# Scan and routing operands in a PSUM bank, one pair of score banks, the third state sum behind qq, and half the zero products

## The chip, the cores and the metric

The program runs on one core of one Trainium2 chip. The metric is the device time of one execution in microseconds (us), 836.23 in the median of three runs (836.04 to 836.23). The clock is that of the whole program: a linear attention, a layer of eight experts behind a router, and a dense feed-forward layer, one after the other.

## The reference

Inputs are q, k, v and alpha of shape (4, 8, 768, 48) and the weights of both layers, all float32.

```python
def _attn_ref(q, k, v, alpha):
    for t in range(S):                       # S = 768 steps, one 48 x 48 state per batch and head
        state = alpha[:, :, t, :, None] * state + einsum('bhd,bhe->bhde', k[:, :, t], v[:, :, t])
        y[:, :, t] = einsum('bhd,bhde->bhe', q[:, :, t], state)

def _moe_ref(x, w_gate, w1, w2):             # x is y as 3072 tokens of 384
    expert_idx = np.argmax(x @ w_gate, axis=1)
    ...                                      # gate_w: softmax probability of the chosen expert
    out[mask] = gate_w[mask, None] * (np.maximum(xe @ w1[e], 0.0) @ w2[e])   # for each of 8 experts

def _moe2_ref(x, w_in, w_out):
    h = np.maximum(x @ w_in, 0.0)
    return h * h @ w_out
```

## The kernel before

**Tiling.** The 32 pairs (batch, head) times two are 16 pairs of heads, and the 768 steps are two halves of three chunks of 128 steps. That makes NU = 32 units; units 0 to 15 are the first halves, units 16 to 31 the second. A tile of one unit is 112 rows (48 of one head at row 0, 48 of the other at row 64) by 3 x 128 steps. The state between chunks is carried by matrices of 112 x 48.

**One unit's work.** `scan` (line 181, VectorE) makes the running products of alpha within each chunk, A; it reads the loaded tile `qka` and `rst`, a tile of 112 x 387 that restarts the product at each chunk and bounds it from below. `prep_a` (188 to 190, ScalarE) makes 1/A as exp(-ln A). `prep_p` (199 and 200, GpSimd from unit 2 on) makes M = k/A and the product R = A/A, from which `prep_k` (205, VectorE) makes the corrected key kk; `prep_q` (210, VectorE) makes qq = q times A. `scores` (225, TensorE) multiplies kk and qq chunk by chunk, `masked` (232, VectorE) applies the causal mask to the product and writes pt. `ktr` transposes kk (241, TensorE; ScalarE copies it to kn, 242). `state_pe` (252, TensorE) makes kn times v per chunk, and `state_0` to `state_4` carry the state through the chunks: `add` (261, VectorE) writes T = product + state, `decay` (257, ScalarE) scales T. The first halves make three sums (called below the first, second and third state sum; a first half's first one needs no addition, so its additions are those of `state_1` and `state_3`), the second halves two. `yout` (289 and 293, TensorE; copy to yt on ScalarE, 295) makes the output, `xout` (312, TensorE) turns it to token rows and adds the router's logits: ScalarE copies the rows (314), VectorE adds the logits (321, 323).

**Zero products.** `fill` issues FILL matmuls of a tile of zeros, 384 columns each, into the score tile ahead of the scores, and into py ahead of `yout`. The real products overwrite them.

**Order.** All engines run the order in which the code is written. In pass u of the loop over units, in the order of the code: kk and qq of unit u+2, scores and transposes of unit u+1, `xout` of unit u-1, mask of u+1, preparation of u+4, `yout` of u, state of u+1, scan of u+5. Every fourth pass from u = 5 on has `route_a` (347 to 359), seven small VectorE instructions that turn logits of four units into one-hot rows and running counts, behind the scan; two passes later `route_b` (368, 369) makes two ranking matmuls and `route_s` the slots to which GpSimd scatters the rows (384). In passes 28 to 30 the first weights of the experts are split into two parts, ScalarE (125) and VectorE (126), at the end of the pass.

**PSUM.** It has eight banks of 512 float32 per row here. The pool `ps_s` has two slots of two banks, tag `sc`, which the score tile takes in turn; the pool `ps_1` has one bank each for `pk`, `st`, `py` and `px`. The router's matmuls share `px`.

Behind the loop the experts and the dense layer run as one dense sequence of matmuls on TensorE (lines 453, 483, 791).

Of the kernel before, what the change touches and what calls it, by code (L numbers as in the profile page):

```python
# [8 lines left out]
F32 = mybir.dt.float32  # L9
# [4 lines left out]
ALU = mybir.AluOpType  # L14
# [6 lines left out]
CH = 128  # L21
# [9 lines left out]
NE = 8  # L31
# [11 lines left out]
CVW = 256  # L43
TINY = 2.0 ** -50
KC = 3
FILL = 2
BLK = 512
PRE = (28, 28, 28, 29, 29, 29, 30, 30)
NBLK = TOK // BLK
# [22 lines left out]
def main_path(tc, qka, v, vt, wg, wts, wf64, cst, out):  # L72
# [24 lines left out]

    def warm(n, pool, tag, x):

        pw = pool.tile([128, 2, 512] if tag == "sc" else [128, 512], F32, tag=tag, name="pw")  # L100
        pw = (pw[:, 0, :] if tag == "sc" else pw)[:, 0:384]
        for _ in range(n):
            nc.tensor.matmul(pw, x[:, 0:128], x[:, 0:384], start=True, stop=True)

# [38 lines left out]

    wi = one.tile([112, NP, 104], F32, name="wi")
    smid = one.tile([112, NPAIR, 48], F32, name="smid")
    rst = one.tile([112, HC, CH + 1], F32, name="rst")
    neg = one.tile([112, 1], F32, name="neg")
    junk = one.tile([112, HC, CH], F32, name="junk")
    zr = one.tile([128, HS], F32R, name="zr")
# [1 line left out]
    tri = one.tile([128, 128], F32R, name="tri")  # L151
    onr = one.tile([128, 128], F32R, name="onr")
    ohx = [one.tile([128, NE, HC + 1], F32R, name=f"ohx{i}") for i in range(2)]
    rone = one.tile([128, NE * (HC + 1)], F32, name="rone")

    st = {}
    SP = ((0, 64), (64, 112))

# [58 lines left out]

    def scores(u):
        kk, qq = st[u, "k"], st[u, "q"]
        sc = ps_s.tile([128, 2, 512], F32, tag="sc", name="sc")  # L220
        fill(sc[:, 0, 0:HS], FILL)
        for j in range(HC):
            cs = slice(j * CH, (j + 1) * CH)
            for x in range(2):
                nc.tensor.matmul(sc[:, x, cs], kk[64 * x:64 * x + 48, cs], qq[64 * x:64 * x + 48, cs], start=True, stop=True, skip_group_check=True)  # L225
        st[u, "sc"] = sc
# [103 lines left out]
    def cv(o):  # L330
        return ct[:, o:o + HC * NE].rearrange("p (i e) -> p i e", e=NE)
# [4 lines left out]
    def col(n):  # L336
        return sm.tile([128, HC, 1], F32, tag=n, name=n)
# [4 lines left out]

    def route_a(g):
        lg = st[g, "lg"]
        mx, wm = col("mx"), col("wm")
        eq, w = t3("eq"), t3("w")
        nc.vector.tensor_reduce(mx, lg, axis=AX.X, op=ALU.max)
        nc.vector.tensor_tensor(eq, lg, bc(mx), op=ALU.is_equal)
        nc.vector.tensor_tensor(w, eq, cv(C_WROW), op=ALU.mult)
        nc.vector.tensor_reduce(wm, w, axis=AX.X, op=ALU.max)  # L350
        oh, ohn = ohx[g % 2], ohx[(g + 1) % 2]
        ohv = oh[:, :, 1:].rearrange("p e i -> p i e")
        nc.vector.tensor_tensor(ohv, w, bc(wm), op=ALU.is_equal)
        cum = sm.tile([128, NE, HC + 1], F32R, tag="cum", name="cum")
        nc.vector.tensor_tensor_scan(cum.rearrange("p e i -> p (e i)"), rone, oh.bitcast(F32).rearrange("p e i -> p (e i)"), 0.0, op0=ALU.mult, op1=ALU.add)
        if g < 2 * B - 1:
            nc.vector.tensor_copy(ohn[:, :, 0:1], cum.bitcast(F32)[:, :, HC:HC + 1])
        else:
            nc.vector.tensor_copy(cnt[:, 0:NE], cum.bitcast(F32)[:, :, HC])
        if g == GA - 1:  # L360
            nc.vector.tensor_copy(cnt[:, NE:NE + 1], cum.bitcast(F32)[:, 0, HC:HC + 1])
        st[g, "rt"] = ohv, cum, mx
# [139 lines left out]
    with tc.manual_schedule():  # L502
        load(0)
        load(1)
        nc.scalar.preload_act_table_set("natural_log_exp_and_others")
        nc.vector.memset(rst, 2.0 ** -60)
        nc.vector.memset(rst[:, :, 0:1], 1.0)
        nc.gpsimd.memset(zt, 0.0)
        nc.gpsimd.memset(zr.bitcast(F32), 0.0)
        nc.gpsimd.memset(neg, -1.0)  # L510
        nc.gpsimd.memset(chk, 0.0)
        nc.gpsimd.memset(wi, 0.0)
        nc.gpsimd.memset(ones, 1.0)
        for u in range(2, 6):
            load(u)
            if u == 2:
                for x in range(2):
                    nc.sync.dma_start(wi[64 * x:64 * x + 48, :, 96:104], wg.rearrange("(p x e) g -> x e p g", p=NP, x=2)[x])
        warm(8, ps_s, "sc", zt)
        scan(0)  # L520
        prep_a(0)
        prep_p(0)
        prep_k(0)
        prep_q(0)
        scan(1)
        prep_a(1)
        scan(2)
        prep_p(1)
        prep_a(2)
        prep_p(2)  # L530
        scores(0)
        ktr(0)
        warm(7, ps_1, "py", zt)
        masked(0)
        prep_k(1)
        prep_q(1)
        scan(3)
        prep_a(3)
        prep_p(3)
        state_pe(0)  # L540
        state_0(0)
        for x, r in enumerate((0, 64)):
            nc.vector.tensor_copy(wi[r:r + 48, :, x * 48:x * 48 + 48], ct[r:r + 48, r:r + 48].rearrange("p (a c) -> p a c", a=1).to_broadcast([48, NP, 48]))
        nc.vector.tensor_copy(tri, ct[:, C_TRI:C_TRI + 128])
        nc.vector.tensor_copy(onr, ones)
        nc.vector.memset(rone, 1.0)
        nc.vector.memset(rone.rearrange("p (e i) -> p e i", e=NE)[:, :, 0:1], 0.0)
        nc.vector.tensor_copy(ohx[0][:, :, 0], ct[:, C_EC:C_EC + 8])
        scan(4)
        xsv = xs.rearrange("(e r) d -> e r d", e=NE)[:, 0:C].rearrange("e (p j) d -> e p j d", p=ZP)  # L550
        nz, ns, ready = 0, 0, 0
        for u in range(NU):
            if u + 6 < NU:
                load(u + 6)
            if u >= 2 and nz < 2 * NE:
                for _ in range(2):
                    nc.sync.dma_start(xsv[nz // 2, :, nz % 2 * 2:nz % 2 * 2 + 2], zt[0:ZP].rearrange("p (j d) -> p j d", j=1).to_broadcast([ZP, 2, XW]))
                    nz += 1
            if u + 2 < NU:
                prep_k(u + 2)  # L560
                state_1(u)
                prep_q(u + 2)
            else:
                state_1(u)
            if u + 1 < NU:
                scores(u + 1)
                ktr(u + 1)
            state_2(u)
            g, gs = divmod(u - NP - 1, NP)
            if u > 0:  # L570
                xout(u - 1)
            if u + 1 < NU:
                masked(u + 1)
            state_3(u)
            if u + 4 < NU:
                prep_a(u + 4)
            state_4(u)
            if u + 4 < NU:
                prep_p(u + 4)
            yout(u)  # L580
            if 14 <= u < 22:
                wload(0, (u - 14) // 4, nc.scalar, (u - 14) % 4)
            rs = gs + (g == 2 * B - 2)
            if g >= 0 and rs == 2:
                route_b(g)
            if u + 1 < NU:
                state_pe(u + 1)
            if u + 5 < NU:
                scan(u + 5)
            if u + 1 < NU:  # L590
                state_0(u + 1)
            if g >= 0 and rs == 2:
                route_s(g)
                ready = g + 1
            if g >= 0:
                if gs == 0:
                    route_a(g)
            for k, x in enumerate(PRE):
                if u == x:
                    split_step(0, k, 8)  # L600
            for _ in range(2 if u >= 28 else 1):
                if u >= 9 and ns < min(ready, GA if u <= 28 else 2 * B) * HC:
                    scatter(ns)
                    ns += 1
            if u == 28:
                assert ns == GA * HC
                xload(0)
                wload(1, 0)
        while ns < ready * HC:
            scatter(ns)  # L610
            ns += 1

        pts = [ps_s.tile([128, 2, 512], F32, tag="sc", name="xt0")[:, 0, :], ps_1.tile([128, 512], F32, tag="st", name="xt1"), ps_1.tile([128, 512], F32, tag="pk", name="xt2")]
        pts = xtr_pe(0, pts)
        fill(banks(0)[0][:, 0:HS], 2)
        xout_a(NU - 1)
        xsp(0, 0, pts[0])
        xsp(0, 1, pts[1])
        xsp(0, 2, pts[2])
        xout_b(NU - 1)  # L620
        st["xl"] = e0p.tile([PARTS[0][3], PARTS[0][2] // PARTS[0][3], NE + 1], F32, name="xl", bufs=1)
        nc.vector.tensor_copy(st["xl"], st["xr", 0][:, :, DM:XW])
        g = 2 * B - 1
        route_a(g)
        g1a(0, 0)
        g1a_pe(0, 1)
        route_b(g)
        route_s(g)
        while ns < 2 * B * HC:
            scatter(ns)  # L630
            ns += 1
        g1a_act(0, 1)
        for npre in range(len(PRE), 10):
            split_step(0, npre, 8)
        npre = max(10, len(PRE))
# [503 lines left out]
```

## Time and profile before

| what | us |
|---|---|
| median of three runs | 836.23 |
| the profiled execution | 836.37 |
| its span from first to last instruction | 834.4 |
| TensorE busy | 819.3 |
| VectorE busy | 570.8 |
| ScalarE busy | 394.5 |
| GpSimd busy | 291.4 |
| units 3 to 30, from the fill of unit 3's scores to that of unit 31's | 30.40 to 168.00 |

The profile has a page of totals and a trace that can be asked for stretches. A row of the time line names the start and the length in us, the engine, the line, the operation, what it writes and reads, and how many such instructions it holds; a bracket gives the idle time of the engine ahead of it and what ended that. Rows of TensorE with several matmuls are pipelined: the start of the next row tells when the engine took up the next work, better than the length does. PE is TensorE, DVE VectorE, ACT ScalarE, POOL GpSimd.

### The profile page before, as it was taken

The numbers are of one execution on the slowest core, as the hardware profiler recorded it, in microseconds if no ns is written. First come the engines' busy times: TensorE is split into PE (matmuls) and PEld (weight loads), VectorE is DVE, ScalarE is ACT, GpSimd is POOL, SyncE is SP. The second block draws the span as 40 slices with busy tenths as digits, with TensorE's granted clock in tenths as the row PEclk, the third lists the DMA queues.
The fourth block names the chain that finished last, engine by engine and source line by source line (L and its number), as shares of the span: only waits on it lengthen the run. The fifth ranks groups of instructions, "written<-read, shape, count | busy, mean of one in ns | idle before, by whom it ended". The sixth has DMA issues, their size and how long they took to land.

```text
span 834.4 us, 14539 instructions
## 1 busy us (share of the span) xinstructions
PE 819.3 (98%) x5412; PEld 731.9 (88%) x5412; DVE 570.8 (68%) x1085; ACT 394.5 (47%) x885; POOL 291.4 (35%) x310
## 2 busy tenths in 40 slices
PE   8999999999999999999999999999999999999996
PEld 5777777789999999999989999999998999999996
DVE  6798999766687898875546878888464444354353
ACT  4666776654454454554434444445363333333332
POOL 2456767630145655530004556563000011011011
PEclk9899999999999999999999999999999999999999
DMA  9795785144856776752523443722423032121111
GB/s 266 240 269 170 205 259 181 55 144 137 284 176 207 233 259 186 240 176 91 183 72 85 119 113 95 228 64 83 139 71 95 1 113 77 39 95 40 57 58 60
DMA packets 56990, 118.12 MB, mean 142 GB/s; under 512 B 12272, under 2 KB 36688, under 8 KB 54608
## 3 DMA queue, kind: packets, MB, share of 16 engines
q1 hardware_dynamic: 52144, 100.59, 39.5%
q0 software_dynamic: 3072, 9.55, 3.1%
q10 hardware_dynamic: 1696, 6.98, 2.6%
q8 instruction: 44, 0.72, 0.4%
q14 instruction: 34, 0.28, 0.1%
HBM read 85.38 MB, written 31.73 MB: 140 GB/s over the span
## 4 chain that ended last, share of the span: by engine, by line
PE 92%; DVE 3%; issue 2%; DMA 1%; ACT 1%; POOL 0%; SPq 0%; POOLq 0%; DVEq 0%; ACTq 0%
PE ph L453 38%; PE bp L791 10%; PE pair L483 9%; PE bpx L791 7%; PE bpy L791 7%; PE third L483 5%; PE sc L225 3%; PE py L289 2%; PE py L293 2%; PE px L312 2%; PE sc L216 2%; PE pst L252 1%; PE pk L241 1%; PE py L216 1%; DMA qka<-qka 1%
## 5 line engine op out<-in xcount | busy, mean ns | idle before, releaser
L774 DVE TENSOR_TENSOR room<-room 128x512 f32<-128x512 f32 (+1 forms) x112 | 77.9, 695 | 148.0 <-ACT room L772 147.9
L772 ACT ACTIVATE room<-ph 128x512 f32<-128x512 f32 (+1 forms) x112 | 60.2, 538 | 235.7 <-PE ph L453 235.6
L824 POOL DMA_INDIRECT out<-room,id x24 | 23.6, 985 | 228.5 <-DVE room L807 223.4
L453 PE MATMUL ph<-xth,w00h 128*128 128x512 f32 (+3 forms) x288 | 102.1, 354 | 0.1
L453 PE MATMUL ph<-xth,w00l 128*128 128x512 f32 (+3 forms) x288 | 100.8, 350 | 0.0
L453 PE MATMUL ph<-xtl,w00h 128*128 128x512 f32 (+3 forms) x288 | 100.2, 348 | 0.0
L453 PE MATMUL ph<-xth,w10h 128*128 128x512 f32 (+2 forms) x264 | 95.6, 362 | 0.0
L453 PE MATMUL ph<-xtl,w10h 128*128 128x512 f32 (+2 forms) x264 | 95.4, 361 | 0.0
L453 PE MATMUL ph<-xth,w10l 128*128 128x512 f32 (+2 forms) x264 | 95.3, 361 | 0.0
L775 DVE TENSOR_TENSOR htl<-room,hth 128x512 fp32r<-128x512 f32 (+1 forms) x112 | 74.2, 662 | 14.5
L721 POOL TENSOR_TENSOR cvg<-cvg,cvd 128x256 f32<-128x256 f32 x48 | 39.8, 829 | 121.0 <-issue 75.6
L726 POOL TENSOR_SCALAR cvc<-cvt 128x256 f32<-128x256 f32 x48 | 38.0, 792 | 102.7 <-DMA cvt<-wf 64.3
L199 POOL TENSOR_TENSOR M<-R,qka 112x384 f32<-112x384 f32 x30 | 46.6, 1552 | 55.7 <-ACT R L189 47.0
L773 ACT ACTIVATE hth<-room 128x512 fp32r<-128x512 f32 (+1 forms) x112 | 64.0, 571 | 3.6
L466 ACT ACTIVATE hth<-ph 128x448 fp32r<-128x448 f32 (+2 forms) x72 | 36.2, 503 | 61.8 <-PE ph L453 59.6
L467 DVE SCALAR_TENSOR_TENSOR htl<-ph,hth 128x448 fp32r<-128x448 f32 (+2 forms) x72 | 40.9, 568 | 30.4 <-ACT hth L466 30.1
L453 PEld LDWEIGHTS ph<-xtl,w00h 128*128 128x128 f32 x288 | 54.2, 188 | 6.7 <-DVE xtl L431 0.2
L453 PEld LDWEIGHTS ph<-xth,w00h 128*128 128x128 f32 x288 | 54.4, 189 | 5.4 <-DVE xtl L431 0.3
L453 PEld LDWEIGHTS ph<-xth,w00l 128*128 128x128 f32 x288 | 54.2, 188 | 4.3
L453 PEld LDWEIGHTS ph<-xtl,w10h 128*128 128x128 f32 x264 | 49.5, 188 | 5.9
L453 PEld LDWEIGHTS ph<-xth,w10h 128*128 128x128 f32 x264 | 49.6, 188 | 4.6
L453 PEld LDWEIGHTS ph<-xth,w10l 128*128 128x128 f32 x264 | 49.6, 188 | 4.5
(215 smaller groups left out, 2144.9 us busy)
## 6 DMA issues: line engine op xcount, KB each, us to landing
wst<-wts SPq DMA_DIRECT2D x14, 1536.0 KB, 6.7
qka<-qka SPq DMA_DIRECT2D x30, 505.3 KB, 4.8
cvt<-wf SPq DMA_DIRECT2D x48, 256.0 KB, 3.7
xb<-x2t SPq DMA_DIRECT2D x10, 768.0 KB, 5.7
wf<-cvg SPq DMA_DIRECT2D x48, 128.0 KB, 3.2
xs<-zt SPq DMA_DIRECT2D x16, 343.9 KB, 7.0
x2t<-ot SPq DMA_DIRECT2D x8, 672.0 KB, 4.4
xr<-xs SPq DMA_DIRECT2D x7, 687.8 KB, 6.0
```

The costliest lines, as they stand in the source:

```text
L199: eng.tensor_tensor(M, R, c3(t[:, HS:2 * HS]), op=ALU.mult)
L453: nc.tensor.matmul(ph, a[:, o:o + 128], x[:, kc, :], start=(k == 0), stop=(k == 8))
L466: nc.scalar.activation(hi, ph, AF.Relu)
L467: nc.vector.scalar_tensor_tensor(lo, ph, 0.0, hi.bitcast(F32), op0=ALU.max, op1=ALU.subtract)
L483: nc.tensor.matmul(acc, a[:, ws], b, start=(f == 0 and i == 0), stop=(f == 7 and i == 2))
L721: nc.gpsimd.tensor_tensor(g, g, cvt.pop((k, "d")).bitcast(F32), op=ALU.mult)
L726: nc.gpsimd.tensor_scalar(c, cvt[k, "t"].bitcast(F32)[:, :, 1], F64_HI, -F64_HI, op0=ALU.min, op1=ALU.max)
L772: nc.scalar.activation(u, ph, AF.Relu)
L773: nc.scalar.activation(hi, u, AF.Square)
L774: nc.vector.tensor_tensor(g, u, u, op=ALU.mult)
L775: nc.vector.tensor_tensor(lo, g, hi.bitcast(F32), op=ALU.subtract)
L791: nc.tensor.matmul(acc, h[:, ts], w[:, ws], start=(f % 8 == 0 and k == 0), stop=(f % 8 == 7 and k == 2))
```

## The change

Five things are changed. FILL goes from 2 to 1. The score tile is allocated once (`sct`), so all units' scores use the same two banks. The other slot of that pool holds `cbank`, one bank that takes `rst` (387 columns), the router's row of weights `crow` (24), `rone` (32) and the router's two maxima `cmx`, `cwm` (3 each); these were SBUF tiles or a part of the SBUF constants. `ktr` is issued behind `state_2`, and `state_3`, the third state sum, moves from behind the mask to the place behind `state_2`, which for VectorE is behind qq and ahead of the logits and the mask. One copy fills `crow` in the prologue.

```diff
-FILL = 2
+FILL = 1
...
-        pw = pool.tile([128, 2, 512] if tag == "sc" else [128, 512], F32, tag=tag, name="pw")
-        pw = (pw[:, 0, :] if tag == "sc" else pw)[:, 0:384]
+        pw = sct[:, 0, 0:384] if tag == "sc" else pool.tile([128, 512], F32, tag=tag, name="pw")[:, 0:384]
...
-    rst = one.tile([112, HC, CH + 1], F32, name="rst")
-    rone = one.tile([128, NE * (HC + 1)], F32, name="rone")
+    sct = ps_s.tile([128, 2, 512], F32, tag="sc", name="sct")
+    cbank = ps_s.tile([128, 2, 512], F32, tag="sc", name="rst")[:, 0, :]
+    rst = cbank[0:112, 0:HA].rearrange("p (c s) -> p c s", c=HC)
+    crow = cbank[:, HA:HA + HC * NE]
+    rone = cbank[:, HA + 24:HA + 24 + NE * (HC + 1)]
+    cmx, cwm = [cbank[:, HA + 56 + k * HC:HA + 56 + (k + 1) * HC].rearrange("p (c e) -> p c e", e=1) for k in range(2)]
...
-        sc = ps_s.tile([128, 2, 512], F32, tag="sc", name="sc")
+        sc = sct
...
-        mx, wm = col("mx"), col("wm")
+        mx, wm = cmx, cwm
...
-        nc.vector.tensor_tensor(w, eq, cv(C_WROW), op=ALU.mult)
+        nc.vector.tensor_tensor(w, eq, crow.rearrange("p (i e) -> p i e", e=NE), op=ALU.mult)
...
+        nc.vector.tensor_copy(crow, ct[:, C_WROW:C_WROW + HC * NE])
...
                 scores(u + 1)
+            state_2(u)
+            if u + 1 < NU:
                 ktr(u + 1)
-            state_2(u)
+            state_3(u)
             g, gs = divmod(u - NP - 1, NP)
             if u > 0:
                 xout(u - 1)
             if u + 1 < NU:
                 masked(u + 1)
-            state_3(u)
```

On VectorE, one pass of the first half stands before as follows (kk is the corrected key, T the state sums, x the logits, pt the masked scores, A the scan).

```order
44 L205 SCALAR_TENSOR_TENSOR kk<-R,M 112x384 [waits Pool_49]
45 L261 TENSOR_TENSOR T<-pst,S 112x48 [waits Activation_49]
46 L210 TENSOR_TENSOR qq<-qka,A 112x384
47 L323 TENSOR_TENSOR x<-px,x 128x3x8 [waits DVE_49,Activation_49]
48 L232 TENSOR_TENSOR pt<-sc,ct 128x768
49 L261 TENSOR_TENSOR T<-pst,S 112x48
50 L181 SCALAR_TENSOR_TENSOR A<-qka,rst 112x387 [waits DMAHW7_49]
```

And so the same pass stands now:

```order
45 L209 SCALAR_TENSOR_TENSOR kk<-R,M 112x384 [waits Pool_49]
46 L265 TENSOR_TENSOR T<-pst,S 112x48 [waits Activation_49]
47 L214 TENSOR_TENSOR qq<-qka,A 112x384
48 L265 TENSOR_TENSOR T<-pst,S 112x48 [waits Activation_49]
49 L327 TENSOR_TENSOR x<-px,x 128x3x8 [waits DVE_49,Activation_49]
50 L236 TENSOR_TENSOR pt<-sct,ct 128x768
51 L185 SCALAR_TENSOR_TENSOR A<-qka,rst 112x387 [waits DMAHW7_49]
```

The second T of the pass, which is the third state sum, has moved from behind pt to behind qq, and has a wait for ScalarE of its own.

On ScalarE, the part of a pass from the output copy yt to the token rows x stands before as follows (S is a scaled state, kn the transposed keys).

```order
51 L295 COPY yt<-py 112x384 [waits PE_49]
52 L257 ACTIVATE S<-pst,A 112x48 [waits PE_49]
53 L242 COPY kn<-pk 128x336 [waits PE_49]
54 L257 ACTIVATE S<-T,A 112x48 [waits DVE_49]
55 L314 COPY x<-px 128x3x96 [waits PE_49]
```

Now:

```order
51 L299 COPY yt<-py 112x384 [waits PE_49]
52 L261 ACTIVATE S<-pst,A 112x48 [waits PE_49]
53 L261 ACTIVATE S<-T,A 112x48 [waits DVE_49]
54 L246 COPY kn<-pk 128x336 [waits PE_49]
55 L318 COPY x<-px 128x3x96 [waits PE_49]
```

The scaling of the second sum, which waits for VectorE, now stands ahead of the copy kn.

On TensorE, the start of a unit's block stands before as follows (zr is the tile of zeros).

```order
64 L216 MATMUL sc<-zr 128x384 x2
65 L225 MATMUL sc<-qq,kk 128x128 x6
66 L241 MATMUL pk<-ct,kk 128x112 [waits PE_49]
67 L241 MATMUL pk<-ct,kk 128x112 x2
68 L312 MATMUL px<-wi,yt 128x104 [waits Activation_49]
69 L312 MATMUL px<-wi,yt 128x104 x2
70 L216 MATMUL py<-zr 112x384 [waits PE_49]
71 L216 MATMUL py<-zr 112x384
```

Now:

```order
60 L220 MATMUL sct<-zr 128x384 [waits DVE_49]
61 L229 MATMUL sct<-qq,kk 128x128 x6
62 L245 MATMUL pk<-ct,kk 128x112 [waits PE_49]
63 L245 MATMUL pk<-ct,kk 128x112 x2
64 L316 MATMUL px<-wi,yt 128x104 [waits Activation_49]
65 L316 MATMUL px<-wi,yt 128x104 x2
66 L220 MATMUL py<-zr 112x384 [waits PE_49]
```

Each of the two groups of zero products has one matmul instead of two, and the one ahead of the scores waits for VectorE: it overwrites banks that the mask of the unit before has to have read.

## Rows read from the trace of the kernel before

**Rows 1.** Stretches: length; busy (count) of PE, PEld, DVE, ACT, POOL; clock; DMA; GB/s.

```profile
22.20:30.40 8.20, 8.20 (x70) 6.57 (x70) 5.24 (x9) 4.25 (x14) 3.05 (x3) 0.58 0.98 309
30.40:95.93 65.53, 62.51 (x747) 48.42 (x746) 59.25 (x116) 45.08 (x146) 41.42 (x32) 1.00 0.73 213
95.93:168.00 72.07, 72.07 (x848) 56.25 (x845) 64.67 (x137) 48.88 (x151) 49.93 (x41) 1.00 0.57 173
```

**Rows 2.** Time line, TensorE: one plain unit of the first half.

```profile
65.12 0.62 PE L216 MATMUL sc<-zr 128*128 128x384 f32 x2
65.67 0.94 PE L225 MATMUL sc<-qq,kk 48*128 48x128 f32 x12
...
67.48 0.58 PE L216 MATMUL py<-zr 128*112 128x384 f32 x2
68.00 0.87 PE L289 MATMUL py<-pt,v 128*64 128x128 f32 x12
...
69.48 0.52 PE L252 MATMUL pst<-v,kn 128*64 128x48 f32 x12
69.93 0.44 PE L216 MATMUL sc<-zr 128*128 128x384 f32 x1
```

**Rows 3.** Time line, the other engines in the same unit.

```profile
65.31 1.30 DVE L205 SCALAR_TENSOR_TENSOR kk<-R,M 112x384 f32<-112x384 f32 x1
...
67.08 0.44 ACT L242 COPY kn<-pk 128x336 f32<-128x336 f32 x1 [1.30 <-PE pk L241]
67.42 0.34 ACT L257 ACTIVATE S<-T,A 112x48 f32<-112x48 f32 x1
...
67.74 0.40 ACT L314 COPY x<-px 128x288 f32<-128x288 f32 x1
...
68.18 0.18 DVE L321 COPY x<-px 128x24 f32<-128x24 f32 x1 [0.38 <-ACT x L314]
68.28 0.95 DVE L232 TENSOR_TENSOR pt<-sc,ct 128x768 f32<-128x768 f32 x1
...
69.14 0.20 DVE L261 TENSOR_TENSOR T<-pst,S 112x48 f32<-112x48 f32 x1
69.26 0.95 DVE L181 TENSOR_TENSOR_SCAN A<-qka,rst 112x387 f32<-112x387 f32 x1
69.30 1.71 POOL L199 TENSOR_TENSOR M<-R,qka 112x384 f32<-112x384 f32 x1 [1.91 <-ACT R L189]
```

**Rows 4.** Time line, second half: GpSimd's M under the mask, and kk alone.

```profile
112.66 0.55 DVE L205 SCALAR_TENSOR_TENSOR kk<-R,M 112x384 f32<-112x384 f32 x1
...
118.35 0.94 DVE L232 TENSOR_TENSOR pt<-sc,ct 128x768 f32<-128x768 f32 x1
...
119.07 1.00 POOL L199 TENSOR_TENSOR M<-R,qka 112x384 f32<-112x384 f32 x1 [1.15 <-ACT R L189]
```

**Rows 5.** Time line around routing: in the first half, and in pass 29.

```profile
52.14 0.55 DVE L205 SCALAR_TENSOR_TENSOR kk<-R,M 112x384 f32<-112x384 f32 x1
...
53.60 0.95 DVE L232 TENSOR_TENSOR pt<-sc,ct 128x768 f32<-128x768 f32 x1
...
54.81 0.52 PE L252 MATMUL pst<-v,kn 128*64 128x48 f32 x12 [0.88 <-DVE T L261]
...
168.34 0.17 DVE L347 TENSOR_REDUCE mx<-x 128x3 f32<-128x24 f32 x1
...
169.77 1.49 DVE L126 TENSOR_TENSOR w00l<-wst,w00h 128x384 fp32r<-128x384 f32 x3
```

**Rows 6.** Time line, unit around the first weight splits.

```profile
163.26 0.62 PE L216 MATMUL sc<-zr 128*128 128x384 f32 x2
...
165.81 0.55 DVE L205 SCALAR_TENSOR_TENSOR kk<-R,M 112x384 f32<-112x384 f32 x1
...
167.99 0.62 PE L216 MATMUL sc<-zr 128*128 128x384 f32 x2
```

**Rows 7.** Time line, TensorE at the start of the loop.

```profile
22.17 0.79 PE L252 MATMUL pst<-v,kn 128*64 128x48 f32 x12 [1.35 <-DVE T L261]
```

## The prediction

> **What bounds the kernel now.** I read the table of stretches first. Behind the loop nothing is changed, so only the first 178 us count. In units 16 to 30 TensorE is busy through the whole 72.07 us, in units 3 to 15 for 62.51 of 65.53 us [rows 1]; VectorE has 59.25 and 64.67 us in them, so it is close behind. The time line of one unit then says what "busy" hides. TensorE's groups follow each other without a gap from one score fill at 65.12 to the next at 69.93, 4.81 us [rows 2]. VectorE in that unit waits 0.38 us ahead of the logits, for ScalarE's copy of the rows [rows 3], and that copy waits for TensorE's px. So TensorE's own work sets a plain unit, and VectorE needs 4.81 - 0.38 = 4.43 us of it. Where routing comes in the first half, VectorE sets the pace: TensorE waits 0.88 us for a state sum before it can start pst [rows 5].
>
> **The zero products.** Two score fills take from 65.12 to 65.67, two output fills from 67.48 to 68.00 [rows 2]. One of each goes: half of 0.55 and half of 0.52, 0.53 us a unit, all on the path. The fills' columns do no other work, and with the group behind them waiting for nothing, no cover is lost. From 30.40 to 168.00 there are 13 and 15 units: 28 x 0.53 = 14.8 us.
>
> **The third state sum.** In a plain unit of the first half it runs from 69.14 to 69.34 and pst starts at 69.48 [rows 2, 3]: TensorE stands 0.14 us behind the sum. Moved behind qq, the sum is done 0.95 us or more earlier and pst comes when its matmuls are issued. What is gained lies between nothing and that 0.14; I take 0.12, because pst follows the sum by the same lag as in the routing unit, where the trace names the sum as what ended the wait. Eight units of the 13 are plain (three have routing, two the ranking matmuls, which stand ahead of pst and cover the wait): 1.0 us.
>
> **Scan operand in PSUM.** The scan itself stays at 0.95 us in my sum. It is GpSimd that changes. M begins 0.04 us behind the scan and takes 1.71 us [rows 3]; an M that begins while the mask runs, which reads one operand from PSUM, takes 1.00 [rows 4]. So a scan with two SBUF operands holds M up, and the mask doesn't. M then holds up kk: 1.30 us behind it [rows 3], 0.55 where nothing of GpSimd is near [rows 4]. With `rst` in PSUM M runs under the scan and is through about when kk is due, so kk takes some 0.7 instead of 1.30. VectorE's need falls from 4.43 to about 3.85.
>
> A page speaks against this step. The Trainium skill (VectorE: DVE Perf Modes, section on the TRN2 errata) gives VectorE a fixed cost of 120 cycles with a PSUM source and 58 without, so by an estimate from that page each moved operand would cost 0.065 us; on seven small routing instructions and a scan in six units that would be some 3 us at most. The trace disagrees: mask (768 columns, PSUM) 0.95 and kk (384, SBUF) 0.55 [rows 3, 4] lie on one line of 1.04 ns a column with the same 0.15 us at its foot.
>
> **One pair of score banks.** This adds a wait: the score fill of the next unit, and all of TensorE behind it, wait for the mask. The mask starts 3.16 us behind its unit's fill, at 68.28 [rows 2, 3]; with one fill less ahead of px 2.89, ends at 3.84, and with 0.14 us of lag the fill may go at 3.98. The unit is now 4.81 - 0.53 - 0.12 = 4.16 us. The wait is hidden by 0.18 us in the first half and by about 0.3 in the second, whose unit is 167.99 - 163.26 = 4.73 [rows 6], then 4.20. It is not hidden where VectorE is late.
>
> *Routing units.* From one mask to the next VectorE has mask 0.87, scan 0.87 (each 0.08 less than its row, since the next starts before the end), routing 1.43 (168.34 to 169.77, a pass in which GpSimd doesn't disturb it), and from kk to the next mask 1.46 (52.14 to 53.60) [rows 5]. In that last stretch ScalarE's scaling follows kk's sum and the row copy follows the scaling; now kn stands between them, 0.34 us from its start to the next [rows 3]. Sum 4.97. The mask begins at 2.89 + 4.97 = 7.86, ends at 8.81, releases at 8.95, which is 4.79 behind the unit's own fill at 4.16: TensorE stalls 0.63. In the three routing units of the first half a stall of 0.88 becomes 0.63, 0.8 us gained. In the three of the second half (passes 17, 21, 25), where two pairs of banks hide the routing today, a stall of about 0.6 is new: 1.8 us lost.
>
> *Weight splits.* In the unit that begins at 163.26 kk starts only at 165.81, 2.55 behind the fill [rows 6], because the splits stand ahead of it. Mask at 2.55 + 1.46 + 0.34 = 4.35, release at 4.35 + 0.95 + 0.14 = 5.44 instead of 4.20: 1.2 us lost.
>
> **The start.** pst of unit 1 waits 1.35 us for the third sum [rows 7], which stands behind a mask of 0.95. I take 1.0 off here, and 0.4 for halved fills in the stretch of lower clock that follows (clock 0.58 on the mean from 22.20 to 30.40 [rows 1]); between 0.5 and 2.5. Nothing is taken for the rest of the prologue, nor for the last two passes, in which TensorE waits for VectorE's splits and slots. No DMA issue changes place. In the busiest 8.2 us the queues moved 309 GB/s at a share of 0.98; the first half moves 213 x 65.53 = 14.0 MB [rows 1], which that rate does in 45 us, below the new 57.
>
> **Sum.** -14.8 - 1.0 - 0.8 + 1.8 + 1.2 - 1.4 = -15.0. On the profiled execution's 836.37 that is 821.4; the median lies 0.14 below it, so 821.2.
>
> **Rivals.**
> *The operand in PSUM changes nothing for GpSimd.* Then the change doesn't do what it says there: VectorE still needs 4.43, more than TensorE's 4.16 and 4.20, and the small routing instructions still meet M, for up to its 1.00 us [rows 4] in six units. 8 x 0.27 + 11 x 0.23 + 6 x 1.0 = 10.7: 832. Against it: M under the mask [rows 4]. For it: no scan with such an operand is in the trace. 0.10.
>
> *The scan becomes fast.* The Trainium skill (Vector Engine (DVE) Microarchitecture Reference, section on points that are easy to get wrong) says that an instruction of this class with two SBUF sources that aren't bf16 runs at half rate; by it one operand in PSUM would free the scan. As a mechanism of this kernel: 387 columns in kk's time, 0.55 instead of 0.95. Plain units gain nothing, since TensorE sets them; the six routing units gain 0.4 each: 818.8, and less where the start gains too. Against it kk, which has two float32 SBUF sources and takes 0.55 for 384 columns [rows 4]: the scan's time is its own. 0.08.
>
> *The single pair of banks binds everywhere.* If R of GpSimd gets ahead of kk, or a release takes longer than 0.14, the mask comes 0.2 to 0.4 late in each unit against a cover of 0.18 to 0.3: up to 0.2 in 28 units, 5.6 us, 826.8. For it: VectorE's order has 0.3 us to spare, no more. 0.15.
>
> *Slower: TensorE's clock falls.* The fills keep TensorE occupied, and halving them with new stalls of 0.6 may let the granted clock drop from 2.4 to 1.2 GHz as it did from 22.20 to 30.40, behind waits of over 1 us [rows 1, 7]. A unit of 4.16 us would take up to 4 more; four such units undo the gain, and ten of 28 give some 846. Against it: the three stalls of 0.88 in the first half left the clock at 1.00 [rows 1, 5], and plain units stay without gaps. 0.04.
>
> **How the numbers follow.** The forecast (818 to 824.5) has 0.61, the rivals 0.10, 0.08, 0.15 and 0.04, and 0.02 that the time stays. The range reaches down to 817, where a fast scan and 2.5 us at the start meet, and up to 828, over the third rival: 0.17 is left out. A change of 0.2% is about what a measurement of this kernel can tell. Faster 0.94, same 0.02, slower 0.04.
>
> **What would show it.** A fill row ahead of scores and of py that is 0.27 long to the next group; plain units of 4.16 and 4.20; M of 1.00 in most units and kk at 0.6 to 0.8; pst no longer waiting for a sum; TensorE waiting for the mask at the score fill by 0.6 in six routing units and by 1.2 once behind 163; scan 0.95. Wrong would be a score fill that waits in plain units, M still at 1.7, or a clock below 1.00 in the loop.

## The result and the profile after

| | before | after | forecast |
|---|---|---|---|
| median | 836.23 | 824.84 (821.04 to 825.06, four runs) | 821.2 |
| ratio, 95% interval | | 0.9846 [0.9827, 0.9866] | |
| profiled execution | 836.37 | 824.76 | 821.4 |
| fill of unit 3 | 30.40 | 29.10 | -1.4 |
| units 3 to 15 | 65.53 | 58.49 | -8.7 |
| units 16 to 30 | 72.07 | 68.57 | -4.95 |

The change is faster by 1.5%, inside the range, and 3.6 us behind the forecast. Its gain is 11.6 us in the profiled executions; 11.8 of it lies ahead of unit 31's score fill, and 0.2 is given back behind that, so the comparison is one of the loop, by the same stretches as [rows 1]. A ratio here and below is taken over the runs and leaves out slow ones, more than 1.5% above the fastest of their kernel, so it can differ from the quotient of the medians. Columns: stretch, its length, busy time (count) of PE, PEld, DVE, ACT, POOL, granted clock, DMA share, GB/s.

```profile
22.20:29.10 6.90, 6.90 (x55) 5.60 (x55) 4.59 (x9) 4.05 (x13) 2.90 (x4) 0.55 0.90 294
29.10:87.59 58.49, 57.73 (x722) 45.71 (x720) 49.93 (x115) 45.32 (x144) 31.32 (x30) 1.00 0.84 245
87.59:156.16 68.57, 67.05 (x815) 53.06 (x815) 59.09 (x139) 49.15 (x153) 42.67 (x41) 1.00 0.59 182
```

TensorE is busy in nearly the whole of both halves, and VectorE has room now: 49.93 of 58.49 us, where it had 59.25 of 65.53. GpSimd's 41.42 us in the first half became 31.32. The lower clock at the start is still there (0.55).

The time line of a plain unit, TensorE first; it answers to [rows 2].

```profile
60.37 0.44 PE L220 MATMUL sct<-zr 128*128 128x384 f32 x1
60.74 0.94 PE L229 MATMUL sct<-qq,kk 48*128 48x128 f32 x12
61.61 0.51 PE L245 MATMUL pk<-ct,kk 112*128 112x112 f32 x3
61.95 0.83 PE L316 MATMUL px<-wi,yt 112*128 112x104 f32 x6
62.55 0.41 PE L220 MATMUL py<-zr 128*112 128x384 f32 x1
62.89 0.87 PE L293 MATMUL py<-pt,v 128*64 128x128 f32 x12
63.69 0.64 PE L297 MATMUL py<-qq,S 48*48 48x128 f32 x8
64.26 0.55 PE L256 MATMUL pst<-v,kn 128*64 128x48 f32 x12
64.74 0.44 PE L220 MATMUL sct<-zr 128*128 128x384 f32 x1
```

No group waits, and the unit takes 64.74 - 60.37 = 4.37 us; 4.16 was forecast. The score fill has 0.37 us to the next group, where the pair had 0.55; the output fill has 0.34, where the pair had 0.52. So the second product of a pair was worth 0.18 us, not half of the pair. The group pst does not wait at 64.26: the third sum, below, is done at 62.71.

The other engines, as in [rows 3] and [rows 5]: the same unit, then a unit behind a routing, then the one with the weight splits.

```profile
59.84 0.95 DVE L185 TENSOR_TENSOR_SCAN A<-qka,rst 112x387 f32<-112x387 f32 x1
59.99 1.00 POOL L203 TENSOR_TENSOR M<-R,qka 112x384 f32<-112x384 f32 x1 [2.36 <-DVE pt L236]
...
60.70 0.70 DVE L209 SCALAR_TENSOR_TENSOR kk<-R,M 112x384 f32<-112x384 f32 x1
...
62.51 0.20 DVE L265 TENSOR_TENSOR T<-pst,S 112x48 f32<-112x48 f32 x1
...
63.25 0.18 DVE L325 COPY x<-px 128x24 f32<-128x24 f32 x1 [0.54 <-ACT x L318]
...
65.42 0.18 DVE L352 TENSOR_TENSOR eq<-x,rst 128x24 f32<-128x24 f32 x1
...
68.44 0.95 DVE L236 TENSOR_TENSOR pt<-sct,ct 128x768 f32<-128x768 f32 x1
...
69.44 0.44 PE L220 MATMUL sct<-zr 128*128 128x384 f32 x1 [0.25 <-DVE pt L236]
...
156.16 0.44 PE L220 MATMUL sct<-zr 128*128 128x384 f32 x1 [0.90 <-DVE pt L236]
```

M takes 1.00 us under the scan instead of 1.71, kk 0.70 instead of 1.30, and VectorE waits 0.54 us in a unit of 4.37 to 4.38: it needs 3.84, and 3.85 was forecast. The single pair of score banks is waited for where the forecast put it, but less: 0.25 behind this routing (0.63 forecast) and 0.90 behind the splits (1.2). The fill starts 0.05 us behind the mask's end (68.44 + 0.95 = 69.39, fill at 69.44), where the forecast had a lag of 0.14.

### The profile page after: what moved, and what is told of

Its sections match the earlier page's. It is cut to its first block, busy times and chain, and to the rows that moved or that the text cites. A ratio compares the mean times of both kernels' runs of the same rounds, so it can differ in the third digit from the quotient of the medians.

```text
span 822.8 us, 14398 instructions
## 1 busy us (share of the span) xinstructions
PE 808.0 (98%) x5348; PEld 725.0 (88%) x5348; DVE 554.6 (67%) x1086; ACT 394.7 (48%) x885; POOL 273.7 (33%) x310
## 4 chain that ended last, share of the span: by engine, by line
PE 88%; DVE 7%; issue 2%; ACT 2%; DMA 0%; POOL 0%; POOLq 0%; DVEq 0%; ACTq 0%
PE ph L457 38%; PE bp L797 10%; PE pair L487 10%; PE bpx L797 7%; PE bpy L797 7%; PE third L487 5%; PE sct L229 2%; PE px L316 2%; DVE pt L236 2%; PE py L293 2%; PE py L297 1%; DVE A L185 1%; PE pk L245 1%; PE sct L220 1%; PE pst L256 1%
## 5 line engine op out<-in xcount | busy, mean ns | idle before, releaser
L203 POOL TENSOR_TENSOR M<-R,qka 112x384 f32<-112x384 f32 x30 | 29.9, 998 | 61.6 <-DVE pt L236 41.9
```

Source lines behind the costliest of these rows:

```text
L203: eng.tensor_tensor(M, R, c3(t[:, HS:2 * HS]), op=ALU.mult)
```

## Experiments

Each kernel was timed beside the kernel before, which stood at 836.57 to 836.94 us in the median, and at 838.32 beside the last. A unit below is the time from one unit's first score product to the next; "first half" is units 3 to 15, "second half" 16 to 30.

**No zero products at all.**

```diff
-FILL = 1
+FILL = 0
```

> The changed kernel with no zero products in the loop at all (FILL 0; the real products overwrite the banks anyway). Theory: a unit of the changed kernel, 4.38 us, is the plain sum of TensorE's groups, of which the one score fill takes 0.37 and the one output fill 0.34; without them TensorE needs some 3.8 to 3.9 (the groups that now follow each other directly keep a change of 0.1 to 0.2), and VectorE needs 4.38 - 0.54 = 3.84. Plain units of 3.85 to 4.05, in all 812 to 816 us. Rival 1 (the fills keep the clock up): the granted clock falls below 1.00 in the loop and the time rises above 824.8. Rival 2 (something other than TensorE sets the 4.38): plain units stay above 4.25, 821 to 825 us.

Measured: 827.43 us in the median of five, with runs from 816.78 (mean clock 0.992) to 839.11 (0.961); 0.9794 [0.9751, 0.9837] without the two at 838.42 and 839.11. The spread goes with the clock: the run at 822.04 has a mean of 0.982, the one at 827.43 has 0.978. The profiled run is the one at 838.42; in it the 1.2 GHz level begins at 21.56 and lasts 54.61 us.

```profile
18.14:21.56 3.42, 1.92 (x30) 1.31 (x31) 3.42 (x7) 2.71 (x9) 2.15 (x3) 0.97 0.76 181
21.56:76.17 54.61, 54.61 (x422) 45.06 (x420) 29.18 (x67) 30.77 (x91) 17.07 (x18) 0.50 0.73 221
```

Ahead of the fall TensorE had work for 1.92 of 3.42 us; then its rows fill the whole stretch, at 6.90 us a unit. At the higher level the plain unit is 3.82. So both things expected come true, each in its stretch: the sum of TensorE's groups goes on falling (to a little below the 3.85 expected), and the lower level, which the changed kernel has for 6.83 us at the same place, stays for eight units here. It comes once more within the loop, in unit 22, which takes 7.60 us.

**One zero product, and nothing else of the change.**

```diff
 (kernel before)
-FILL = 2
+FILL = 1
```

> The kernel before with FILL 1 and nothing else. Theory: the second of two zero products costs 0.18 us in each group (its weight load hides under the first), not half of the pair: second-half units 4.73 - 0.36 = 4.37, first-half plain units 4.81 - 0.36 = 4.45 with the wait for the third sum still in them, in all 836.2 - 28 x 0.36 = 826 us, so that all other parts of the change bring 1 to 2 us together. Rival (each is worth half of its pair, and the missing 3.6 us are lost in a wait that the other edits bring): units of 4.20 and 4.28, 821 us.

Measured: 835.51 us (829.78 to 840.75, ten runs), 0.9981 [0.995, 1.0012]: nothing in the median. The two runs with a mean clock of 0.995 took 829.78 and 830.79, some 6 us less than the kernel before; the others, at 0.992 down to 0.981, took 832.68 to 840.75. At the higher clock the plain units of the first half take 4.64 and routing units 5.65 as before, since pst now waits for the state sum:

```profile
PE pst L252 <- DVE T L261: 5.0, 10, 1.2
```

(in us: total, number of times and longest, from 30 to 95 us). What the second half would gain (4.38 a plain unit) went into the clock. In the profiled run it fell for 13.65 us at 94.88, where units take 7.3 to 7.6, and for 6.83 us at 176.8. So the largest edit brought its gain only together with the others: with them neither that wait nor the fall within the loop is there. Which of the waits brings the fall is not separated. The theory's unit of the second half was right, its 4.45 for the first half and its 826 were not.

**The scan's operand back in SBUF.**

```diff
-    rst = cbank[0:112, 0:HA].rearrange("p (c s) -> p c s", c=HC)
+    rst = one.tile([112, HA], F32, name="rsts").rearrange("p (c s) -> p c s", c=HC)
```

> The changed kernel with the operand rst of the scans back in SBUF; the router's operands stay in PSUM. Theory: M of GpSimd that starts under a scan takes 1.7 us again, kk 1.3, and VectorE needs some 4.43 us a unit, more than TensorE's 4.38: plain units 4.43 to 4.55, in all 826 to 830 us. Rival (with TensorE at 4.38 the scan's operand is idle talk): plain units 4.38 and the time within 1 us of 824.8, whatever M takes.

Measured: 825.98 us (825.53 to 827.36), 0.9876 [0.9856, 0.9897]. Plain units stay at 4.37. Units behind a routing go from 4.70 to 4.95 in the first half and stand at 4.81 to 4.87 in the second (4.50 to 4.90 in the changed kernel); the loop is 128.32 instead of 127.05 us. M takes 1.60 and kk 1.29 us again, as expected, but the plain unit does not grow, so VectorE's need there is no more than TensorE's 4.37, and not the 4.43 of the theory. The scan's operand in PSUM matters behind the routings alone, 1.3 us in the loop.

**ktr ahead of state_2 again.**

```diff
-            state_2(u)
             if u + 1 < NU:
                 ktr(u + 1)
+            state_2(u)
             state_3(u)
```

> The changed kernel with the transposes of kk (and their copy kn on ScalarE) ahead of the scaling of the second sum again; the third sum stays behind qq. Theory: kn of 0.34 us leaves the chain from kk to the mask in routing units and in the unit behind the first weight split, where TensorE waits for the mask (0.1 to 0.5 in six units, 1.0 once): 1 to 2 us less, 823 to 824 us. Rival (the scaling of the second sum, now behind kn, comes too late for the third sum or for the output products): plain units longer than 4.38, 825 us or more.

Measured: 820.98 us (819.80 to 825.53), 0.9828 [0.9792, 0.9864]. Units behind a routing take 4.37 to 4.56 instead of 4.50 to 4.90, the unit with splits 5.10 instead of 5.34, the loop 125.17 instead of 127.05. The copy kn, which the change put between state scaling and row copy, costs the 0.34 us that the forecast had put there, 1.9 us in all. The rest of the gain lies ahead of the loop: in the profiled run the lower clock at the start did not come, and the fill of unit 3 stands at 26.78 instead of 29.10.

```profile
18.40:21.80 3.40, 1.65 (x26) 0.92 (x24) 3.29 (x9) 2.84 (x11) 2.09 (x2) 1.00 0.59 167
21.80:28.60 6.80, 6.55 (x86) 5.20 (x82) 6.51 (x12) 4.83 (x18) 4.02 (x4) 1.00 0.90 270
```

The run at 825.53 has a mean clock of 0.990, the three others 0.995 to 0.998; where the clock was lower in runs without a profile is not known.

**Zero products in TensorE's waits of pass 0,** on top of that.

```diff
+        spare = ps_1.tile([128, 512], F32, tag="px", name="spare")[:, 0:HS] if u == 0 else None
+        if u == 0:
+            fill(spare, 3)
         for c in range(1 - h, HC):
+            if u == 0 and c == 2:
+                fill(spare, 4)
...
+        if u == 0:
+            fill(spare, 3)
```

> ktr ahead of state_2 as in the run before, and ten more zero products in pass 0, written into the bank of px (not used yet there) in TensorE's waits for kk, the masked scores and yt. Theory: the lower clock at the start of the loop (6.83 us at the 1.2 GHz level in the changed kernel) follows those waits of TensorE, and with them filled no run has it: granted clock 1.00 from the first units on, every run near 820 (819 to 822), unit 3 to 31 at 125.2 us as before this edit. Rival: the drop has nothing to do with TensorE's waits: it comes in some runs as without the edit, and these read 824 to 826; or the ten products, 0.3 us each at most, come on the path: up to 3 us more.

Measured: 820.08 us, 819.29 to 820.31, all four runs at a mean clock of 0.998; 0.9798 [0.9782, 0.9814]. The same stretch, columns as above, of the changed kernel and of this one:

```profile
18.34:21.76 3.42, 1.45 (x23) 0.82 (x21) 3.42 (x7) 2.53 (x9) 2.15 (x3) 0.98 0.69 186
21.76:28.59 6.83, 6.83 (x43) 5.40 (x43) 4.64 (x9) 4.13 (x15) 2.89 (x3) 0.51 0.90 280
```

```profile
18.40:21.80 3.40, 3.40 (x28) 2.11 (x26) 3.40 (x7) 2.82 (x9) 2.40 (x3) 1.00 0.62 167
21.80:28.60 6.80, 6.80 (x88) 5.53 (x89) 6.47 (x12) 4.79 (x18) 3.75 (x4) 1.00 0.96 294
```

TensorE has work for all of the 3.40 us, the clock stays at the 2.4 GHz level, and twice as many matmuls go through the next 6.8 us. Of the nine traces of kernels that leave these waits open, the kernel before included, eight have the fall between 21 and 24 us, with 0.87 to 2.05 us of TensorE's work in the 3.4 us ahead of it; the run with ktr first is the one without (1.65 us of work in 3.40, clock 1.00, above). Of the five with filled waits none has it. So the fall came only behind TensorE's waits in pass 0, and not each time.

**The third sum back behind the mask** (ktr ahead of state_2 as well, so the order is that of before).

```diff
-            state_2(u)
             if u + 1 < NU:
                 ktr(u + 1)
-            state_3(u)
+            state_2(u)
...
                 masked(u + 1)
+            state_3(u)
```

> The changed kernel with the third state sum back behind the mask and ktr back ahead of state_2; one zero product of each group, the operands in PSUM and the single pair of score banks stay. Theory: in the first half VectorE's mask then stands ahead of the sum for which pst waits. With the unit shortened the wait is no longer 0.14 but 0.3 to 0.4 us: plain units of the first half 4.64 instead of 4.38, units with routing 5.3 to 5.6 instead of 4.70, together 4 to 6 us in 13 units; second half 4.38 as in the changed kernel, since it has no third sum. 829 to 832, and more if waits of that size let the clock fall within the loop as they did with one zero product in the kernel before. Rival: what held up the first half was kk beside M, which the operand in PSUM has cured; the place of the sum is worth the 1.0 us that the forecast took for it: 825 to 826.

Measured: 826.23 us (823.62 to 827.44), 0.987 [0.9844, 0.9897]. Plain units of the first half take 4.64, and its time line says why:

```profile
59.76 0.95 DVE L236 TENSOR_TENSOR pt<-sct,ct 128x768 f32<-128x768 f32 x1
...
60.63 0.20 DVE L265 TENSOR_TENSOR T<-pst,S 112x48 f32<-112x48 f32 x1
...
60.97 0.52 PE L256 MATMUL pst<-v,kn 128*64 128x48 f32 x12 [0.22 <-DVE T L265]
```

The sum behind the mask makes pst wait 0.22 us here. Beside the run with ktr first, which differs in the sum's place alone, the first half is 61.02 instead of 57.49 us and the second the same (67.66 and 67.68): the moved sum is worth 3.5 us. Routing units take 4.86, less than the 5.3 to 5.6 expected, and the total is below 829 because this run has ktr in its cheaper place, which the expectation left out.

**Operands in SBUF, two pairs of banks.**

```diff
-    sct = ps_s.tile([128, 2, 512], F32, tag="sc", name="sct")
-    cbank = ps_s.tile([128, 2, 512], F32, tag="sc", name="rst")[:, 0, :]
+    cbank = one.tile([128, 512], F32, name="rst")
...
-        sc = sct
+        sc = ps_s.tile([128, 2, 512], F32, tag="sc", name="sc")
```

> The changed kernel with its operands of scans and routing back in SBUF and two pairs of score banks, so that no score fill waits for a mask; one zero product of each group and the moved sum stay. Theory: a plain unit is TensorE's own sum in both, 4.37; the single pair costs up to 0.6 us in each of six units with routing and 1.0 in the unit with the weight splits, and the operands in PSUM save about as much in the same units: 824 to 827, both halves within 1 us of the changed kernel. Rival: the single pair is the dearer of the two, and without it the six units with routing and the one with splits fall to 4.4 and 4.4: 2 to 3.5 us less, 821 to 823.

Measured: 828.63 us (827.16 to 835.71, eight runs, the two above 835 at a mean clock of 0.984), 0.9928 [0.9899, 0.9957]; both expectations were too low. The unit with splits falls to 4.38, 0.96 us better, but a routing unit and the next one together take 9.8 to 10.2 us, where the changed kernel has 9.2 to 9.6. The loop is 130.11 us, 3.1 more. VectorE and GpSimd at a routing:

```profile
64.23 1.60 POOL L203 TENSOR_TENSOR M<-R,qka 112x384 f32<-112x384 f32 x1 [1.59 <-DVE pt L236]
...
65.14 0.73 DVE L352 TENSOR_TENSOR eq<-x,rst 128x24 f32<-128x24 f32 x1
...
66.34 0.58 DVE L357 TENSOR_TENSOR ohx<-w,rst 128x24 fp32r<-128x24 f32 x1
```

With two SBUF operands the scan goes together with an M of 1.60 instead of 1.00, as in the kernel before; beside M then eq takes 0.73, against 0.18 in the changed kernel, and beside R ohx takes 0.58. The Trainium skill (SBUF — State Buffer, section "SBUF: two separate sides") says that VectorE with two SBUF inputs and GpSimd take a shared pair of ports as a lock, for the whole instruction; these rows agree: eq ends 0.04 us behind M (65.14 + 0.73, 64.23 + 1.60). The run turns two things at once, the operands and the pair of banks; the operands in PSUM together with two pairs would need nine of the eight banks, so their prices are told apart only by place, the splits for the pair and the routings for the operands.

**Which zero product is worth what.** Three kernels, the last two on top of the one with filled waits in pass 0: two products again; none ahead of the output from unit 4 on; none ahead of the scores from unit 4 on.

```diff
 (1) FILL = 1  ->  FILL = 2
 (2)
-        fill(py, FILL)
+        fill(py, FILL if u < 4 else 0)
 (3)
-        fill(sc[:, 0, 0:HS], FILL)
+        fill(sc[:, 0, 0:HS], FILL if u < 4 else 0)
```

> The changed kernel with two zero products in each group, as before; all other edits stay. Theory: the second product of a group is worth 0.18 us, so a plain unit goes from 4.38 to 4.73; in the six units with routing and the one with splits the longer unit hides the mask's release, so they gain less than 0.36: some 8 to 9 us in 28 units, 833 to 834. Rival (the forecast's value): half of a pair, 0.27 a product, unit 4.91, 839 or more.

> As the run with filled waits in pass 0, and from unit 4 on without the zero product ahead of the output; the one ahead of the scores stays. Theory: that product is worth 0.34 us a unit until the single pair of score banks binds: the mask of a plain unit releases them 4.07 us behind the unit's own fill, so plain units go from 4.38 to 4.07, 27 x 0.3 = 8 us less: 811 to 814, with the clock at 1.00. Rival: the zero products keep TensorE busy enough for the higher clock, as the run without any showed: with half of them gone the clock falls for stretches of 6.83 us or more, each costing about 2.5 to 3 us, and the time lies at 820 or above.

> As the run with filled waits in pass 0, and from unit 4 on without the zero product ahead of the scores; the one ahead of the output stays. Theory: a zero product is worth its columns wherever it stands, 0.18 us, since the end of the group ahead of it hides the rest: units 4.19 as in the run that left out the other one, 817 to 818, clock 1.00. Rival: its row is 0.37 long to the next group, and it is worth that: units 4.01, 813.

Measured: (1) 832.79 us (829.85 to 834.06), 0.9941 [0.9922, 0.996], plain units 4.72: two products cost 0.35 us in a plain unit, 0.175 each. The loop takes 134.64 instead of 127.05 us, 7.6 more and not 28 x 0.35, since the longer unit covers the wait for the mask: 4.72 behind a routing too. (2) 817.43 us (817.34 to 817.76), 0.9769 [0.9753, 0.9785], plain units 4.19: 0.18 for the only product ahead of the output, not 0.34, and so 3 to 6 us above what was expected. (3) 813.01 us (812.65 to 813.66), 0.9718 [0.9699, 0.9738], plain units 4.00: 0.37 for the only one ahead of the scores. The mean clock is 0.996 and above in all runs of (2) and (3). The rows ahead of the output in (2), then those ahead of the scores in (3):

```profile
58.09 0.83 PE L323 MATMUL px<-wi,yt 112*128 112x104 f32 x6
58.85 0.87 PE L293 MATMUL py<-pt,v 128*64 128x128 f32 x12
```

```profile
59.20 0.55 PE L256 MATMUL pst<-v,kn 128*64 128x48 f32 x12
59.68 0.94 PE L229 MATMUL sct<-qq,kk 48*128 48x128 f32 x12
```

Without a zero product px has 0.76 us to the next group, with one 0.60 (61.95 to 62.55 above): its end lay under the product. pst has 0.48 with one and without. So 0.175 to 0.18 is what the product itself takes in both groups, and the first product ahead of the scores brings 0.19 more. The theory for (3), the same price everywhere, was wrong; the row's length to the next group was right there.

**No zero product from unit 4 on,** on top of the filled waits in pass 0 (edits 2 and 3 together).

> As the run with filled waits in pass 0, and no zero products at all from unit 4 on. Theory of the sum: TensorE's own work is then 3.82 in the first half and 4.02 in the second, and VectorE's mask releases the banks some 4.0 behind a unit's own fill: about 4.0 a unit, 0.2 to 0.3 less than with one product a unit, 811 to 813. Theory of the clock: without any zero product TensorE stands waiting in most units and at the 1.2 GHz level for stretches of 3.4 us and longer, as in the run without any: 820 to 840, and far apart from run to run.

Measured: 810.31 us in the median; 809.20, 809.45 and 811.18 at a mean clock of 0.996 to 0.998, and one run of 817.41 at 0.988; 0.9713 [0.9665, 0.9761]. Plain units take 3.82, and units behind a routing 4.5 to 4.7; the next unit's scores wait 0.47 to 0.58 for the mask there, 0.68 in unit 31. The loop stays at the higher clock in the profiled run, although no unit from 4 on has zero products; the start has no open waits in this kernel. The run at 817.41 has no profile, so where its clock was lower is not known.

**Zero products in the waits alone:** the same kernel with two zero products ahead of the scores of units 8, 12, ... 28 and four at unit 31, written into the bank of pk.

```diff
+        if u > 4 and u % 4 == 0 or u == 31:
+            fill(ps_1.tile([128, 512], F32, tag="pk", name="spare")[:, 0:HS], 4 if u == 31 else 2)
```

> As the run without zero products from unit 4 on, but in the units whose scores wait for the mask behind a routing (8, 12, ... 28) two zero products, and at unit 31 four, are written ahead of the scores into the bank of pk, which is free then, so that they run inside the wait. Theory: the one run in four that stood at 817.4 with a mean clock of 0.988 lost it to the clock behind these waits of 0.5 to 0.8 us; with the waits filled every run stands at 809 to 811.5, mean clock 0.996 and above, and the loop is as long as without them (4.5 us in a unit with routing). Rival: plain units without zero products leave TensorE too little to do, so that some runs stand at 816 or above as before; or the products come behind the mask's release instead of inside the wait, 0.37 us in each of six units: 812 to 813.

Measured: 820.12 us (817.72 to 820.71), 0.9775 [0.9756, 0.9794], mean clock 0.988 in four of five runs. The products cost nothing where they stand (4.51 to 4.55 a routing unit, at unit 23 4.75, as without them), and they did not help: the clock fell at the end of the loop and once more behind it.

```profile
139.35:142.76 3.41, 1.94 (x31) 1.33 (x32) 2.76 (x8) 2.13 (x8) 0.00 (x0) 0.99 0.33 91
142.76:149.59 6.83, 6.83 (x46) 5.56 (x44) 4.72 (x15) 2.98 (x8) 0.00 (x0) 0.50 0.00 0
...
156.42:166.66 10.24, 10.24 (x47) 10.24 (x48) 4.84 (x19) 2.60 (x7) 2.26 (x2) 0.50 0.45 182
```

The wait ahead of the first fall is not one of those filled: TensorE waits 1.47 us for a scaled state in the unit with the splits, where the run before waited 0.32. It began with two engines that stood, ScalarE ahead of yt and VectorE ahead of a state sum; TensorE's px, which reads that yt, starts 0.06 us behind its end:

```profile
137.90 0.48 ACT L308 COPY yt<-py 112x384 f32<-112x384 f32 x1 [2.50 <-PE pst L258]
...
138.44 0.92 PE L325 MATMUL px<-wi,yt 112*128 112x104 f32 x6 [0.49 <-issue]
138.68 0.21 DVE L267 TENSOR_TENSOR T<-pst,smid 112x48 f32<-112x48 f32 x1 [2.19 <-PE pk L247]
...
142.19 0.42 PE L304 MATMUL py<-qq,S 48*48 48x128 f32 x4 [1.47 <-ACT S L263]
```

The matmuls of pst, which the state sum reads and which follow those of py, end at 136.74, so the releasers named don't account for starts at 137.90 and 138.68. The cause stays open, and with it whether the run of 817.41 without these products had the same one.

## Why the prediction was right, and where its sum was off

The kernels make a ladder in the first half, each with one line more of the change, all at the higher clock:

| kernel | units 3 to 15 | step |
|---|---|---|
| before | 65.54 | |
| one zero product | 63.39 | -2.15 |
| and operands in PSUM, single pair | 61.02 | -2.37 |
| and the third sum behind qq | 57.49 | -3.53 |
| and ktr behind state_2: the change | 58.49 | +1.00 |

**The zero products: the term that was mis-sized.** 28 x 0.53 was taken as half of each pair of rows. The product that goes is the second, and it measured 0.175 to 0.18, 0.35 a unit (4.73 to 4.38 in the second half): by that the sum would have had 9.8 instead of 14.8 us. It was read from a row that holds both products, and the product that is left takes more than half of it: 0.37 of 0.55 and 0.34 of 0.52. The Trainium skill (TensorE: Matmul & The Clock Gate, section "Back-to-back issue gap") gives the gap behind a matmul as about its columns at 2.4 GHz, by an estimate from that page 0.16 us for 384. The second products measured a little above that.

**The third sum: right in kind, its price another.** Alone it was priced at 0.12 us in eight plain units. On the shorter unit its wait is 0.27 in eight plain units and 0.49 in three with routing, 3.5 us, as the run with the sum back shows. The two edits share one gain: halving the products without moving the sum gives 2.15 us in the first half. The forecast had both together and lost nothing by it, but its price would have been wrong for either alone.

**Scan operand in PSUM: right.** M 1.00, kk 0.60 to 0.71 in most units that are not behind a routing (1.03 to 1.26 in five of the second half), scan unchanged at 0.95, VectorE's need 3.84. The run with the scan's operand in SBUF shows that this is worth nothing in a plain unit and some 0.25 us at most routings; with the routing's operands in SBUF as well, and two pairs of banks, a routing costs 0.5 to 0.9 us more. The rivals of a useless operand (832) and of a fast scan (818.8) are both out.

**One pair of score banks: right in kind, dearer in the forecast.** The wait came in the routing units and behind the splits: units of 4.70 in the first half (4.79 forecast), 4.50, 4.90 and 4.57 in the second, where 4.8 was forecast, and 5.34 (5.44). The longer unit hides 0.2 of it, and the lag behind the mask is 0.05 instead of 0.14. In plain units the fill does not wait, so the rival that it binds everywhere (826.8), near as its time is, is out. With ktr ahead of state_2 the routing units take 4.37 to 4.56: most of what the wait costs there is the place of ktr.

**The start.** 1.3 instead of 1.4 us, but not as it was added up: pst of unit 1 comes 1.24 us earlier (20.93 instead of 22.17, its wait 0.48 instead of 1.35), where 1.0 was taken, and the stretch of lower clock behind it gives 0.05, where 0.4 was taken.

```profile
20.93 0.52 PE L256 MATMUL pst<-v,kn 128*64 128x48 f32 x12 [0.48 <-DVE T L265]
```

The lower clock there was taken as given; in all traces that have it, it stands behind TensorE's waits, and it is worth 3 to 4 us: the stretch of 6.83 us holds 43 matmuls where the run with filled waits has 88, and the one run of the changed kernel with a mean clock of 0.998 took 821.04 us, the others, at 0.994 and 0.995, 824.76 to 825.06 (of these four only one at 0.994 has a profile).

**The clock in the loop.** The slower rival did not come, as the granted clock of 1.00 in both halves shows. It is no idle fear: halving the products alone brought it in, between 0.981 and 0.995 of mean clock in ten runs. The units at the lower level took 7.3 to 7.6 us there, some 3 more than at the higher; the rival put 4 at most, and its 846 for ten units goes by 2.5 each.

**The sum.** With the measured size of the product it is -15.0 + 5.0 = -10.0. The routing units and the one with splits came out 2.2 us better than forecast (1.0 in the first half, 1.2 in the second), the other terms 0.6 worse, of which 0.2 behind the loop: -11.6. So the total came as near as it did partly by luck: an overpriced gain was met by an overpriced loss, and the two hang together, since the longer unit is what hides the wait for the mask.

## What to carry to other kernels

A row that holds two instructions is not two halves: what goes with one of them is what the second adds, and a run with one more or one fewer tells its price. Edits that shorten TensorE's unit and edits that take waits out of it share a gain, and one without the other can give nothing, by the clock too (835.51 us with one zero product alone). The version to keep is the one without the score fills, with ktr in its old place and filled waits in pass 0: 812.65 to 813.66 us in four runs, against 836.6; without any zero product from unit 4 on it is 809 to 811 in three runs of four, and 817 in the fourth.

## What the runs showed of the hardware

- TensorE stayed at the 1.2 GHz level for 54.61 us although its rows fill that stretch; in the changed kernel, whose rows fill the stretch too, the level lasted 6.83 us. The Trainium skill (TensorE: Matmul & The Clock Gate, section "What's actually happening") says that activity releases the throttle; that these groups, whose rows have no gap, did not release it in 54.61 us is not in line with it. The ends of these rows are modelled, so they do not show how busy the engine was within them.
- A zero product of 384 columns cost 0.175 to 0.18 us behind another and behind px, and 0.37 as the only one between pst and the scores (plain units of 4.72, 4.37, 4.19 and 4.00). Why the last is dearer stays open.
- Small VectorE instructions with two SBUF operands took 0.58 to 0.73 us beside GpSimd, and 0.18 to 0.20 with one operand in PSUM.
